# Moving the range check of 16 weight pieces from the last layer into attention

## The chip, the cores and the metric

The kernel runs on one core of a Trainium2 chip. The time is the device time of one execution in microseconds, as the median of several runs. TensorE does the matrix products, VectorE, ScalarE (ACT in the profile) and GpSimd (POOL) work on elements, and SyncE (SP) issues nearly all transfers between HBM and the chip's memory (SBUF).

## What is computed

Three layers, one behind the other, on 4 x 576 tokens of width 512. The weights w_in and w_out of the last one arrive as float64.

```
# 1. attention: 4 batches, 8 heads, head_dim 64; heads 0-3 see the last 32 keys,
#    heads 4-7 every fourth key of the last 128
scores = where(mask, q @ k.T / 8, -1e9);  x = softmax(scores) @ v
# 2. soft mixture of 8 experts, 4 slots each
logits = x @ phi
slots  = softmax(logits, over tokens).T @ x
out_e  = relu(slots_e @ w1[e]) @ w2[e]
x = softmax(logits, over slots) @ out
# 3. the layer the change is about: w_in 512 x 2048, w_out 2048 x 512
h = x @ w_in;  y = (h - tanh(h)) @ w_out
```

## The kernel before, in words

**Pieces.** w_in and w_out are cut into 16 pieces each, i0 to i15 and o0 to o15: 128 x 512 float64 words, 512 KB. A piece is loaded raw and turned into float32 by three steps on its raw bits: `top` (L276) and `low` (L273), on GpSimd or ScalarE, write the two halves of each word into the piece's place in SBUF; `merge` (L281, VectorE) joins them with bits of the raw word. Both `top` and `low` must be done before `merge`.

**Attention** (`attention`, to about 125 us) goes over 38 batches of four score blocks. Batch k runs `scores(k)`: sixteen matmuls (L466), then mask and row maximum (L470) and subtraction (L474, L477) on VectorE; one batch later `flip` transposes it on TensorE (L485) and ScalarE takes the exponential; another batch later come the product with v (L496) and, on VectorE, `norm` (L512 to L528). `turn` (TensorE, L382 and L394) and `regroup` (GpSimd, L331) prepare q and k of later heads, `shift_v` (GpSimd, L361) v; the logits of layer 2 are summed on VectorE (L430, L432). The order is written out by hand, and each engine takes its instructions in that order.

The first 16 pieces, PRE = i0, o0, i1, ... o7, are prepared in here, one per two batches: in batch 2n piece n is asked for, `top` and `low` follow in batch 2n + 4, and `merge` at the head of batch 2n + 6, ahead of that batch's mask. Their raw words lie in three buffers (`rawx`), so the load of piece n + 3 waits until piece n is merged. Their places are in `pre`. Two places in the loop close a pool and load weights w1, w2 into the room: the first one once all turns of q, k and e are done, the second in batch 36.

**Dispatch, experts and combine** (to about 200 us) stream 32 MB of w1 and w2.

**The last layer** (`second`) is ordered by a planner (`Plan`): every step has an engine, a guessed time and its predecessors, and the steps are written out in the order of the planned starts. It prepares the other 16 pieces and runs eight phases of products over 18 tiles of 128 tokens: h (L1109), its square (L1113, ScalarE), the product r (L1120 on VectorE, or L1124 and L1128 over ScalarE and GpSimd), and the accumulation into acc (L1082).

**The range check.** The fast way is right only for weights within a range. `check` (L890, L892) goes over the top 16 bits of each word of a raw piece and collects a mark: one 128 x 512 array `seen`. At the end `sift`, `marks` and `judge_o` turn it into part of a flag; if the flag is set, a general path (`any_size`) computes the last layer anew. Two pieces, i8 and i9, are checked behind their merge in the last layer. The raw words of the other 30 are gone by then, so the planner loads them a second time (into 12 buffers of the pool `raw`) and checks them one after another. Each check reads the `seen` that the one before wrote.

## Time and profile before

| | |
|---|---|
| median of three runs | 315.47 us (313.72 to 318.79) |
| the profiled execution, its own time | 317.44 us |
| its span, first to last instruction | 315.6 us |
| TensorE busy | 288.0 us, 91% |
| VectorE busy | 223.4 us, 71% |
| ScalarE busy | 157.6 us, 50% |
| GpSimd busy | 150.8 us, 48% |
| loads of raw pieces | 62, of 512 KB each |
| read from HBM | 80.64 MB |

One execution is profiled. PE is TensorE's matmul, PEld its weight load, DVE is VectorE. "a<-b x3" names what is written and read, and how often; "idle before" is the time an engine stood still ahead of the instruction, with what ended it. Matmuls overlap and their ends are modelled, so TensorE's busy time is not its work at full speed. Timeline rows are start us, us, engine, line, operation, [idle before]. Rows of windows give the stretch, its length, the busy us (instructions) of PE, PEld, DVE, ACT and POOL, then PEclk, the clock granted to TensorE as a share of full speed, the DMA engines' busy share and GB/s. Rows of groups end with "busy us, mean ns of one | idle before".

### The profile page before, as it was taken

Reading aid. Unit: us, or ns where it says so; the run is one execution under the profiler, and the core shown is the slowest. Engines: PE = TensorE matmul, PEld = TensorE weight load, DVE = VectorE, ACT = ScalarE, POOL = GpSimd, SP = SyncE. Lnnn points to the kernel's source line nnn. Section 1 sums busy time; section 2 is a strip of 40 time slices with the busy share of each in tenths; the row PEclk is TensorE's granted clock in tenths of the full one; section 3 lists DMA queues with packets and bytes.
Section 4 is the critical chain, followed back from the end, with each engine's and each line's share of the span. In section 5 each row is a group of like instructions: output and inputs, shape, how many; then the busy total and the mean of one; then the engine's idle time right before and its main releaser. Section 6 shows DMA issues by size and latency. Waiting matters only on the chain.

```text
span 315.6 us, 7494 instructions
## 1 busy us (share of the span) xinstructions
PE 288.0 (91%) x2674; PEld 200.0 (63%) x2674; DVE 223.4 (71%) x729; ACT 157.6 (50%) x298; POOL 150.8 (48%) x218
## 2 busy tenths in 40 slices
PE   5899998998899999889999697899999999999990
PEld 3688886786687866644432144556775788787860
DVE  4468896874879886608520026799889998999980
ACT  3366564544263356312310017689785735778630
POOL 8648757755678660010507006979534112433310
PEclk9999999999999999999999899699999999999997
DMA  7989899879797899978999999999445989613004
GB/s 194 257 222 348 227 326 344 267 224 310 235 330 243 287 339 412 384 262 321 374 334 410 409 379 367 387 380 353 158 135 194 312 273 346 207 61 104 31 1 143
DMA packets 61644, 85.93 MB, mean 272 GB/s; under 512 B 18976, under 2 KB 47008, under 8 KB 61600
## 3 DMA queue, kind: packets, MB, share of 16 engines
q1 hardware_dynamic: 60512, 85.12, 80.4%
q8 instruction: 23, 0.38, 0.5%
q10 hardware_dynamic: 1088, 0.26, 0.4%
q14 instruction: 21, 0.17, 0.2%
HBM read 80.64 MB, written 4.72 MB: 270 GB/s over the span
## 4 chain that ended last, share of the span: by engine, by line
PE 51%; DMA 25%; DVE 10%; POOL 5%; ACT 3%; issue 3%; SPq 1%; ACTq 0%; POOLq 0%
PE acc L1082 21%; DMA raw_i<-in_moe_w_in 10%; DMA raw_o<-in_moe_w_out 6%; DMA w<-in_moe_w 6%; PE h L1109 5%; PE sc L466 3%; PE hp L821 2%; PE pv L496 2%; PE pp L485 2%; DVE sm L470 2%; DVE pre L281 2%; POOL pre L273 2%; DMA q<-in_q 2%; POOL pre L276 1%; PE sp L743 1%
## 5 line engine op out<-in xcount | busy, mean ns | idle before, releaser
L1082 PE MATMUL acc<-wh,r 128*128 128x512 f32 x288 | 78.6, 398 | 0.7 <-DVE r L1120 0.7
L1113 ACT ACTIVATE u<-h,co 128x512 f32<-128x512 f32 (+1 forms) x80 | 49.2, 647 | 25.1 <-PE h L1109 20.0
L1082 PEld LDWEIGHTS acc<-wh,r 128*128 128x128 f32 x288 | 53.2, 189 | 13.3 <-issue 2.1
L1128 POOL TENSOR_TENSOR r<-d,u 128x512 fp32r<-128x512 f32 (+1 forms) x22 | 28.8, 1307 | 49.0 <-ACT d L1124 21.3
L1120 DVE SCALAR_TENSOR_TENSOR r<-h,co,u 128x512 fp32r<-128x512 f32 (+1 forms) x58 | 38.4, 691 | 2.6 <-PE acc L1082 1.5
L466 PE MATMUL sc<-kT,qT 64*64 64x96 f32 (+1 forms) x608 | 34.2, 252 | 0.7 <-DVE kT L403 0.4
L470 DVE CUSTOM_DVE_ANT_0 sm<-sc,m_sb 128x96 f32<-128x96 f32 x144 | 29.2, 257 | 7.7 <-PE sc L466 7.7
L486 ACT ACTIVATE pT<-pp 96x512 f32<-96x512 f32 x38 | 23.1, 609 | 21.4 <-PE pp L485 21.4
L466 PEld LDWEIGHTS sc<-kT,qT 64*64 64x64 f32 x608 | 26.9, 133 | 5.0 <-issue 1.8
L361 POOL TENSOR_SCALAR vw<-vw 32x256 f32<-32x256 f32 (+1 forms) x40 | 27.2, 680 | 4.8 <-DMA vw<-in_v 1.4
L1109 PE MATMUL h<-cT,Gs 128*128 128x512 f32 (+1 forms) x80 | 28.6, 394 | 0.5 <-DVE r L1120 0.4
L485 PE MATMUL pp<-c_sb,sm 128*96 128x128 f32 x152 | 23.7, 278 | 3.9 <-DVE sm L474 2.5
L496 PE MATMUL pv<-vw,pT 97*64 97x65 f32 x608 | 26.1, 227 | 0.1
L496 PEld LDWEIGHTS pv<-vw,pT 97*64 97x64 f32 x608 | 20.8, 137 | 7.8 <-issue 6.4
L821 PE MATMUL hp<-w,phi_sb 128*32 128x512 f32 x120 | 22.0, 614 | 3.7 <-DMA w<-in_moe_w 3.3
L404 ACT COPY qT<-tr_q 128x512 f32<-128x512 f32 x16 | 13.6, 853 | 23.5 <-PE tr_q L394 23.5
L474 DVE TENSOR_TENSOR sm<-sm,mx 128x384 f32<-128x384 f32 (+1 forms) x38 | 22.9, 602 | 1.2
L822 DVE COPY store<-hp 128x512 f32<-128x512 f32 x8 | 5.5, 690 | 23.9 <-PE hp L821 17.2
L485 PEld LDWEIGHTS pp<-c_sb,sm 128*96 128x96 f32 x152 | 15.9, 126 | 8.0 <-DVE sm L474 3.4
L420 ACT COPY xT<-xt 128x512 f32<-128x512 f32 (+1 forms) x19 | 14.5, 788 | 11.6 <-PE xt L411 11.0
L1109 PEld LDWEIGHTS h<-cT,Gs 128*128 128x128 f32 x80 | 15.1, 191 | 7.4 <-DVE r L1120 2.4
L822 ACT COPY store<-hp 128x512 f32<-128x512 f32 x8 | 4.7, 583 | 25.8 <-PE hp L821 25.8
(212 smaller groups left out, 513.7 us busy)
## 6 DMA issues: line engine op xcount, KB each, us to landing
w<-in_moe_w SPq DMA_DIRECT2D x58, 512.0 KB, 8.1
raw_o<-in_moe_w_out SPq DMA_DIRECT2D x32, 512.0 KB, 6.6
raw_i<-in_moe_w_in SPq DMA_DIRECT2D x30, 512.0 KB, 7.5
q<-in_q SPq DMA_DIRECT2D x16, 256.0 KB, 5.2
k<-in_k SPq DMA_DIRECT2D x16, 256.0 KB, 5.2
out<-X SPq DMA_DIRECT2D x14, 256.0 KB, 4.4
X<-in_moe_w SPq DMA_DIRECT2D x6, 512.0 KB, 7.1
vw<-in_v SPq DMA_DIRECT2D x16, 144.0 KB, 4.5
```

Of the source, the lines that this page charges most:

```text
L361: copy = lambda dst, src: nc.gpsimd.tensor_scalar(out=dst, in0=src, scalar1=1.0, scalar2=0.0, op0=ALU.mult, op1=ALU.add)
L466: nc.tensor.matmul(dst[half, lo:hi], lhsT=qT[u % NQ][half, i:i + QB], rhs=keys[half], start=True, stop=True)
L470: nc.vector.tensor_tensor_reduce(out=sm[:, o:o + n, :].rearrange("p g k -> p (g k)"), in0=sc[:, o:o + n, :].rearrange("p g k -> p (g k)"), ...
L485: nc.tensor.transpose(pp[:, i, :], sm[:, i, :], ident)
L486: nc.scalar.activation(out=pT[0:KB], in_=pp, func=AF.Exp, scale=0.125)
L496: nc.tensor.matmul(pv[64 * ab:64 * ab + 64, i, :], lhsT=pT[:, o + x, 64 * ab:64 * ab + 64], rhs=w[:, ab, u % 2, j + x, :], start=x == 0, s ...
L821: nc.tensor.matmul(hp[32 * dc:32 * dc + 32, :], lhsT=siT[:, dc, :], rhs=w_sb[8 * e + dc][:, 512 * hf:512 * (hf + 1)], start=True, stop=Tru ...
L1082: nc.tensor.matmul(live[key], lhsT=lhsT(), rhs=rhs(), start=new, stop=n == due)
L1109: nc.tensor.matmul(live["h", key], lhsT=Gs[:, 128 * f:128 * (f + 1)], rhs=cT[:, c0:c0 + w], start=True, stop=True)
L1113: nc.scalar.activation(out=live["u", key], in_=live["h", key], func=AF.Square, scale=co[:, SC, f:f + 1])
L1120: nc.vector.scalar_tensor_tensor(out=live["r", key], in0=live["h", key], scalar=co[:, BB, f:f + 1], in1=live["u", key], op0=ALU.add, op1=A ...
L1128: nc.gpsimd.tensor_tensor(out=live["r", key], in0=live["d", key], in1=live["u", key], op=ALU.mult)
```

## The change

The 16 pieces of PRE are checked in attention, each directly behind its merge and from the raw words that lie there. `check` moves out of `second` and is shared; the two places that call it in the last layer stay. The planner leaves out what was counted already: 16 of the 30 second loads and 16 of the 30 checks. The operation on a piece is the same, except that the first one of all is now i0 and no longer i8.

The mark needs a place before `chk` exists. `places` is a list of buffers; a check writes the newest and reads the one that the check before wrote. The first buffer is the place of the last piece, o7, which is filled only in batch 34. When the first pool is closed in the loop, a buffer of 1 KB per partition (`seen`, in a new pool between `wright` and the next weights) takes over, and in `second` the old one in `chk`.

```diff
@@ -280,6 +280,20 @@
         hi = raws[piece].bitcast(I32).rearrange("p (x two) -> p x two", two=2)[:, :, 1]
         nc.vector.scalar_tensor_tensor(out=w, in0=hi, scalar=3, in1=w, op0=ALU.logical_shift_left, op1=ALU.bitwise_xor)
 
+    places, counted = [], []
+
+    def marked(pool):
+        places.append(pool.tile([128, 512], U16, name=f"seen{len(places)}"))
+        return places[-1]
+
+    def check(piece):
+        x = quarter(piece, 3, U16)
+        if not counted:
+            nc.vector.tensor_scalar(out=places[-1], in0=x, scalar1=0x7800, scalar2=0x3800, op0=ALU.bitwise_and, op1=ALU.bitwise_xor)
+        else:
+            nc.vector.scalar_tensor_tensor(out=places[-1], in0=x, scalar=0x3800, in1=counted[-1][1], op0=ALU.bitwise_xor, op1=ALU.bitwise_or)
+        counted.append((piece, places[-1]))
+
     x0 = ctx.enter_context(tc.tile_pool(name="x0p", bufs=1)).tile([128, 2, NB, DM // 2], F32, name="X0")
     octx = ExitStack()
     xpool = octx.enter_context(tc.tile_pool(name="xpool", bufs=1))
@@ -566,6 +580,7 @@
                         later.append((u + 5, nm))
                 return done
 
+            places.append(place(PRE[-1]).bitcast(U16)[:, 0:512])
             load_qk(0, "e", nc.scalar)
             load_qk(0, "q")
             load_qk(0, "k")
@@ -615,11 +630,14 @@
                 n = k_ // 2
                 if k_ % 2 == 0 and 0 <= n - 3 < len(PRE):
                     merge(PRE[n - 3])
+                    check(PRE[n - 3])
                 if k_ % 2 == 0 and 0 <= n < len(PRE):
                     w_in_out(PRE[n], rawx.tile([128, 512], I64, tag="x", name=f"raw_{PRE[n][0]}{PRE[n][1]}"))
                 for at, cx, n in ((None, rctx, 4), (6 + 2 * (len(PRE) - 1), xctx, 3)):
                     if k_ > 0 and len(early0) == (at is not None) and (not ms and not qk and not later and not [e for e in extras if e[2] is turn] if at is None else k_ >= at):
                         cx.close()
+                        if at is None:
+                            marked(wctx.enter_context(tc.tile_pool(name="seen", bufs=1, side="right", reuse_waits="tile")))
                         early0.append(mctx.enter_context(tc.tile_pool(name=f"early{n}", bufs=n, side="right", reuse_waits="tile")))
                         for _ in range(n):
                             w_load(early0[-1])
@@ -879,18 +897,10 @@
         batches = [[0], [1], [2, 3, 4], [5, 6, 7], [8, 9, 10], [11, 12, 13], [14, 15]]
         joints = [[0], [1], [2, 3, 4], [5, 6, 7], [8, 9, 10], [11, 12, 13, 14, 15]]
         flat = x0.rearrange("p r j d -> p (r j d)")
-        seen = chk.tile([128, 512], U16, name="seen")
-        counted = []
+        seen = marked(chk)
 
         def load(piece):
             w_in_out(piece, raw.tile([128, 512], I64, tag="raw", name=f"raw_{piece[0]}{piece[1]}"))
-
-        def check(piece):
-            if not counted:
-                nc.vector.tensor_scalar(out=seen, in0=quarter(piece, 3, U16), scalar1=0x7800, scalar2=0x3800, op0=ALU.bitwise_and, op1=ALU.bitwise_xor)
-            else:
-                nc.vector.scalar_tensor_tensor(out=seen, in0=quarter(piece, 3, U16), scalar=0x3800, in1=seen, op0=ALU.bitwise_xor, op1=ALU.bitwise_or)
-            counted.append(piece)
 
         for piece in loads[:RAW]:
             load(piece)
@@ -1256,7 +1266,7 @@
 
         ck = None
         for piece in PRE + loads:
-            if piece in counted:
+            if piece in [x[0] for x in counted]:
                 continue
             key = ("raw", ("again", piece))
             ld = add(one("DMA", DMA, lambda piece=piece: load(piece)), deps=[P["mg", loads[-1]]], take=[key])
```

## Rows read from the trace of the kernel before

**Rows 1.** Windows by stretch, busy us (instructions), PEclk, DMA share, GB/s

```profile
26.00:118.00 92.00, 87.73 (x1326) 69.93 (x1320) 73.41 (x373) 46.32 (x94) 65.66 (x103) 1.00 0.92 288
...
140.00:150.00 10.00, 10.00 (x88) 3.95 (x86) 6.54 (x13) 2.38 (x4) 1.31 (x4) 1.00 0.75 271
...
160.00:180.00 20.00, 16.66 (x107) 5.22 (x104) 2.41 (x6) 1.55 (x3) 5.86 (x14) 0.97 1.00 383
...
200.00:210.00 10.00, 9.23 (x42) 6.47 (x43) 8.35 (x16) 7.45 (x15) 7.67 (x10) 0.86 1.04 391
210.00:220.00 10.00, 9.52 (x48) 6.63 (x47) 9.84 (x18) 8.00 (x14) 9.36 (x15) 1.00 1.05 364
...
250.00:260.00 10.00, 10.00 (x47) 8.16 (x46) 9.53 (x16) 4.50 (x8) 2.62 (x2) 1.00 0.93 293
```

**Rows 2.** Chain of waits in order of time: start, us, what

```profile
272.42 2.31 PE acc L1082 x10
```

**Rows 3.** Groups of TensorE's matmuls by line and shape, 248 to 307 us

```profile
L1082 PE MATMUL acc<-wh,r 128*128 128x512 f32 x190 | 50.9, 394 | 0.0
L1109 PE MATMUL h<-cT,Gs 128*128 128x512 f32 x37 | 14.0, 404 | 0.0
L1082 PE MATMUL acc<-Ms,cT 128*128 128x512 f32 x18 | 5.8, 401 | 0.0
```

**Rows 4.** The checks from 220 us on: two groups, then the first one

```profile
L892 DVE SCALAR_TENSOR_TENSOR seen<-raw_o,seen 128x512 uint16<-128x512 uint16 x16 | 16.2, 1015 | 0.3
...
L892 DVE SCALAR_TENSOR_TENSOR seen<-raw_i,seen 128x512 uint16<-128x512 uint16 x14 | 10.9, 778 | 0.2
...
226.47 0.68 DVE L892 SCALAR_TENSOR_TENSOR seen<-raw_i,seen 128x512 uint16<-128x512 uint16 x1
```

**Rows 5.** VectorE's waits, 26 to 118 us: total us, times, longest

```profile
DVE pre L281 <- POOL pre L273: 12.3, 9, 3.3
```

**Rows 6.** Timeline of all engines around one merge, 76 to 80 us

```profile
76.93 0.69 DVE L281 SCALAR_TENSOR_TENSOR pre<-raw_i,pre 128x512 int32<-128x512 int32 x1 [3.34 <-POOL pre L273]
76.97 1.13 POOL L331 TENSOR_SCALAR qm<-q 128x512 f32<-128x512 f32 x1
...
77.54 0.25 DVE L470 CUSTOM_DVE_ANT_0 sm<-sc,m_sb 128x96 f32<-128x96 f32 x1
...
78.07 0.62 POOL L331 TENSOR_SCALAR km<-k 128x512 f32<-128x512 f32 x1
...
78.81 0.47 DVE L477 TENSOR_SCALAR sm<-sm,mx 128x192 f32<-128x192 f32 x1
...
79.33 0.17 PEld L485 LDWEIGHTS pp<-c_sb,sm 128*96 128x96 f32 x2 [0.22 <-DVE sm L477]
```

**Rows 7.** Timelines of VectorE, then TensorE's weight loads, at three merges

```profile
28.67 0.72 DVE L474 TENSOR_TENSOR sm<-sm,mx 128x384 f32<-128x384 f32 x1
...
39.71 0.56 DVE L474 TENSOR_TENSOR sm<-sm,mx 128x384 f32<-128x384 f32 x1
...
117.74 0.42 DVE L432 TENSOR_TENSOR LT<-LT,lp 128x256 f32<-128x256 f32 x1
...
30.21 0.45 PEld L485 LDWEIGHTS pp<-c_sb,sm 128*96 128x96 f32 x4
...
40.38 0.39 PEld L485 LDWEIGHTS pp<-c_sb,sm 128*96 128x96 f32 x4
...
118.21 0.42 PEld L411 LDWEIGHTS xt<-c_sb,X 128*128 128x128 f32 x4 [0.65 <-DVE LT L432]
```

**Rows 8.** Timeline of VectorE, then of GpSimd, at 270 to 280 us

```profile
277.68 2.39 DVE L892 SCALAR_TENSOR_TENSOR seen<-raw_i,seen 128x512 uint16<-128x512 uint16 x2
...
273.87 1.30 POOL L1128 TENSOR_TENSOR r<-d,u 128x512 fp32r<-128x512 f32 x1 [1.54 <-ACT d L1124]
277.69 1.83 POOL L1128 TENSOR_TENSOR r<-d,u 128x512 fp32r<-128x512 f32 x1 [2.52 <-ACT d L1124]
```

**Rows 9.** Timeline of SP's queue, 80 to 90 us

```profile
84.56 0.38 SPq L251 DMA_DIRECT2D raw_o<-in_moe_w_out  x1
```

## The prediction

> **What bounds the kernel now.** I read the page's busy shares first, then the windows by stretch, then the chain of waits, and last the timeline around single merges.
>
> On the page TensorE is busy for 91% of the span and VectorE for 71% (the table above). The average hides three stages. In attention (26 to 118 us) TensorE is busy for 87.73 of 92 us and VectorE for 73.41, so VectorE has 18.6 us to spare; the DMA engines are at 0.92 [rows 1]. In the experts' stretch the transfers of weights set the pace: at 160 to 180 us the DMA engines are full and TensorE idles for 3.3 of 20 us [rows 1]. In the last layer (from 200 us) VectorE looks like the limit, with 9.84 of 10 us busy at 210 to 220 us and 9.53 at 250 to 260, but at 250 to 260 TensorE has no gap at all [rows 1].
>
> Whether TensorE is really full there, its busy time can't say, since the ends of matmuls are modelled. The chain of waits can: ten accumulating matmuls take 2.31 us, 0.231 each [rows 2]. Between 248 and 307 us there are 190 + 37 + 18 of that width [rows 3]; 245 x 0.231 is 56.6 us, and 8 half-wide ones and three small groups add about 1.5. That is 58.1 of 59 us. So the last layer is bound by TensorE's own work to within 1 us, and after the last matmul only copies and stores follow.
>
> In attention the order is another. A batch goes scores (TensorE), mask, maximum and subtraction (VectorE), transpose (TensorE), and TensorE has only about one batch of other work between. What VectorE puts ahead of a batch's mask is on TensorE's path as soon as the slack of that batch is used up. The merges sit exactly there.
>
> **The change, part by part.**
>
> *Removed from the last layer: 16 checks.* The 30 checks there take 16.2 + 10.9 us [rows 4], 0.90 each, so 16 are 14.5 us of VectorE. The first of them runs at 226.5 us [rows 4]. By then TensorE is full, and the most that shorter waits can give back is the 1.0 us of bubbles found above. I take 0.5, the middle of 0 and 1.0.
>
> *Removed: 16 loads of 512 KB*, 8.4 MB on SP's queue. They are issued behind all first-time loads and share the queue with the stores of the outputs; 14 loads of the same kind remain and fill the same buffers first. No TensorE work waits for them. Cost nothing, gain nothing; it would be a gain only if a first-time load or one of the last stores stood behind them.
>
> *Moved: the mark.* Three buffers and no copy: each check writes the newest buffer and reads the one before. No instruction is added. The new 1 KB buffer lies between two pools of weights and shifts the later ones by 1 KB, so that a weight load may wait for another old tile; all those tiles come free in the same two batches. Nothing.
>
> *Added to attention: 16 checks*, each right behind a merge. No row of attention has a check. The nearest row is the merge itself, which has the same form (scalar_tensor_tensor, two inputs in SBUF, 128x512): it starts at 76.93, and the next VectorE instruction at 77.54 [rows 6], so 0.61 us is the low price. The high price comes from GpSimd. Its qm copy, started in the middle of that merge, takes 1.13 us, where the same copy of km behind it takes 0.62 [rows 6]. In the last layer two checks run back to back from 277.68 and take 2.39 us, with a GpSimd multiply beside them that takes 1.83, against 1.30 for one without [rows 8]. So the first check holds the multiply up for 0.5 us, and then the multiply holds the second check for about 1.1 us. A check behind a merge is this second one whenever GpSimd has work waiting, and it mostly has: the helper's next copy starts within 0.1 us of the merge in ten cases. The copy ends at 78.10, 0.56 after the merge, so the high price is 0.61 + 0.54 = 1.15 us. I take 0.88, midway, since GpSimd is busy for 65.66 of 92 us [rows 1] and not every check finds it pending.
>
> The Trainium skill says this as a rule (SBUF — State Buffer, "Who interferes with whom"): a VectorE instruction with two SBUF inputs and a GpSimd instruction that reads SBUF exclude each other, and the later one waits for the whole of the earlier one. The two checks at 277.68 agree. By the rule alone every check would have the high price, the third rival below.
>
> *What of it reaches TensorE.* For each of the 16 merges I compared the end of the batch's last VectorE step with the start of the TensorE step that reads it. At 39.71 + 0.56 = 40.27 the subtraction ends and its transpose loads at 40.38: 0.11 us of slack [rows 7]. At 78.81 + 0.47 = 79.28 the transpose follows at 79.33 [rows 6]. At the last merge it is the logits' sum, 117.74 + 0.42 = 118.16, against 118.21 [rows 7]. Eleven merges are tight like this (at 37.8, 43.2, 50.0, 61.3, 76.9, 83.3, 89.9, 95.0, 105.6, 110.3 and 115.8 us), with 1.18 us of slack in all. The other five have 0.7 to 1.0; the first is 28.67 + 0.72 = 29.39 against 30.21, 0.82 [rows 7].
>
> At 0.61 the tight ones cost 11 x 0.61 - 1.18 = 5.5 us and the others nothing. At 1.15 they cost 11.5, and the others 1.4 beyond their slack: 12.9. At 0.88 it is 8.5 + 0.3 = 8.8 us.
>
> Against that stands what can absorb it. VectorE waits 12.3 us in front of nine merges for GpSimd's two steps of the same piece [rows 5], which wait for the piece's transfer. If that chain (SP's queue, the transfers, GpSimd) keeps its own pace, a batch that is late simply waits less at the next such merge. In the limit only the last merge's cost is left, 0.6 us. But the chain doesn't run free: SP also waits for buffers that TensorE and GpSimd release, and GpSimd loses 0.5 us to each check. I take half of 8.8 us, 4.4, and keep 0.6 to 12.9 for the range.
>
> *Who waits for the waiting instruction.* Behind the check on VectorE stand the masks, the normalization and the copies of logits. SP waits for the check where it waited for the merge, since the raw buffer comes free 0.6 us later; the next load into it is issued 7 to 14 us after the merge in all thirteen cases (the merge at 76.93 ends at 77.62 [rows 6], the load at 84.56 [rows 9]), so that costs nothing. If SP ran closer, each load would go 0.6 us later.
>
> *What follows attention.* The weights of the experts are loaded into places that dispatch and the experts release, and the DMA engines are at 0.75 at 140 to 150 us [rows 1], so they can't run ahead: I pass the delay on in full.
>
> *Sum.* The profiled execution took 317.44 us, 1.84 more than its span. 317.44 + 4.4 - 0.5 = 321.3. It lies 1.97 above the median of the three runs, so on the median's scale the forecast is 319.4 us, 1.2% above 315.47. Two per cent, about what a measurement of this kernel can tell from no change, is 6.3 us.
>
> **The rivals.**
>
> *The waits absorb it.* The transfers keep their own pace, and every late batch is caught at the next merge that waits for GpSimd. For it: nine such waits, the longest 3.34 us [rows 6], and DMA engines at 0.92. Against it: three of the last eight merges have no such wait, and GpSimd is itself pushed. It gives a slip of 0.6 to 2.7 us; with 1.5 and 0.5 back, 316.5.
>
> *Nothing absorbs it.* The copies behind a late GpSimd hold up SP's loads of q and k, these the next raw piece, and the whole chain moves with VectorE, at the high price: 12.9 - 0.5, 327.9 us. For it: the checks at 277.68 and GpSimd at 71% busy. Against it: VectorE's 18.6 us to spare.
>
> *Faster: the last layer gives back more than attention pays.* The place is 200 to 220 us, where TensorE is short of 0.77 and 0.48 us [rows 1] with VectorE at 9.84 of 10. If the planner, freed of 16 checks, puts the products r earlier there, those 1.25 us and the 1.0 us of bubbles come back; with a slip of 0.6 us that is -1.7, 313.8 us. It decides from the point at which the slip is under 2.3 us. Against it: no removed check runs before 226.5 us [rows 4].
>
> *The change doesn't do what it says.* The first mark lies in the place of piece o7, which GpSimd fills in batch 34. The move depends on the last turn of q, k and e, which the code's order puts into batch 32, so batch 33 switches and batch 34's check already writes the second buffer. Were the move a batch later, the mark would hold foreign words, the flag would be set, and the general path would run: its 864 products alone are 864 x 0.231 = 200 us more, over 510 us.
>
> **How the numbers follow.** Forecast (net +2 to +8 us) 0.50; absorbed (-0.5 to +2) 0.22; nothing absorbs (+8 to +13) 0.15; faster 0.11; mark lost 0.02. The range 313.0 to 325.0 takes in the forecast, the absorbed case, most of the faster one and the lower end of the unabsorbed. Slower by over 2% (over 321.8 us, net over 6.3): a fifth of the forecast, 0.10, and 0.15 and 0.02: 0.27. Faster by over 2% would need 6.3 us, which no case but a rest of the third reaches: 0.04. Within: 0.69.
>
> **What would show it.** In the profile after: 16 checks on VectorE between 26 and 120 us, those behind a merge with GpSimd pending at 1.1 us or more, the others at 0.7; longer GpSimd copies; longer waits of transposes for VectorE; the last scores some 4 us later; 46 instead of 62 loads of pieces; VectorE below 9 of 10 from 230 us while the matmuls there keep their 0.231 us. I am wrong if the last scores come at the old time, if the stretch from 220 us to the last matmul shortens by more than 1.4 us, or if the experts' stretch swallows the delay.

## The result and the profile after

The changed kernel takes 319.31 us, the median of five runs (318.67 to 322.37); the kernel before takes 315.47 us in five runs timed beside it (313.72 to 318.79). The ratio is 1.0147 with a 95% interval of 1.0108 to 1.0186: 3.4 to 5.9 us slower, clear of the scatter and inside the two per cent. The profiled execution of the changed kernel is its slowest run, 322.37 us with a span of 320.6.

The windows by stretch of the changed kernel, with the columns of [rows 1]:

```profile
26.00:118.00 92.00, 83.51 (x1267) 67.24 (x1265) 87.21 (x371) 43.61 (x90) 66.13 (x102) 1.00 0.91 279
...
210.00:220.00 10.00, 9.15 (x50) 5.70 (x48) 9.63 (x21) 8.87 (x16) 7.63 (x14) 1.00 1.06 378
250.00:260.00 10.00, 10.00 (x44) 7.74 (x43) 9.90 (x15) 6.16 (x11) 1.50 (x1) 1.00 0.12 46
...
280.00:290.00 10.00, 10.00 (x43) 7.70 (x42) 7.70 (x17) 6.58 (x11) 2.73 (x3) 1.00 0.00 0
290.00:300.00 10.00, 10.00 (x45) 7.86 (x44) 6.72 (x19) 7.77 (x14) 3.90 (x3) 1.00 0.33 107
```

In attention VectorE's busy time rises from 73.41 to 87.21 us of 92, and TensorE's falls from 87.73 to 83.51: TensorE now waits where VectorE waited. At 250 to 260 us nothing has changed: TensorE has no gap, and VectorE is at 9.90 with the checks that are left. Only from 280 us is VectorE below 8 of 10, and TensorE has no gap there either.

The groups of VectorE's instructions in attention, 20 to 124 us, that belong to a merge (L281) or to a check:

```profile
L294 DVE SCALAR_TENSOR_TENSOR pre<-raw_o,pre 128x512 uint16<-128x512 uint16 x7 | 7.9, 1126 | 0.0
L281 DVE SCALAR_TENSOR_TENSOR pre<-raw_i,pre 128x512 int32<-128x512 int32 x8 | 6.8, 854 | 0.0
L294 DVE SCALAR_TENSOR_TENSOR pre<-raw_i,pre 128x512 uint16<-128x512 uint16 x6 | 6.7, 1110 | 0.0
L281 DVE SCALAR_TENSOR_TENSOR pre<-raw_o,pre 128x512 int32<-128x512 int32 x8 | 6.3, 783 | 0.0
...
L292 DVE TENSOR_SCALAR pre<-raw_i 128x512 uint16<-128x512 uint16 x1 | 1.0, 1000 | 0.0
...
L294 DVE SCALAR_TENSOR_TENSOR seen<-raw_i,pre 128x512 uint16<-128x512 uint16 x1 | 0.7, 684 | 0.0
L294 DVE SCALAR_TENSOR_TENSOR seen<-raw_o,seen 128x512 uint16<-128x512 uint16 x1 | 0.7, 683 | 0.0
```

Sixteen checks take 16.9 us, 1.06 each, against the 0.88 that the forecast took. Four of them (74.02, 80.17, 116.47 and 121.47 us) take 0.68 or 0.69, the low price; one takes 0.88, and eleven take 1.00 to 1.53. The four are just those at whose start no GpSimd instruction was running; at the other twelve one was. The timeline of all engines at one merge shows why:

```profile
59.70 0.68 DVE L281 SCALAR_TENSOR_TENSOR pre<-raw_o,pre 128x512 int32<-128x512 int32 x1
59.86 1.16 POOL L273 TENSOR_SCALAR pre<-raw_i 128x512 int16<-128x512 uint16 x1
...
60.30 1.20 DVE L294 SCALAR_TENSOR_TENSOR pre<-raw_o,pre 128x512 uint16<-128x512 uint16 x1
...
61.11 1.13 POOL L375 TENSOR_SCALAR vw<-vw 32x256 f32<-32x256 f32 x2
...
61.43 0.24 DVE L484 CUSTOM_DVE_ANT_0 sm<-sc,m_sb 128x96 f32<-128x96 f32 x1
```

GpSimd's `low` step starts during the merge and runs to 61.02. The check, which has the form of the merge and could run in 0.68 us, ends only at 61.50, half a microsecond behind GpSimd, and the mask (L484) that TensorE needs starts only at 61.43, 1.73 us after the merge began. In [rows 6] it started 0.61 us after.

Who waits for that? TensorE's weight loads, 20 to 124 us of the changed kernel (total us, times, longest):

```profile
PEld pp L499 <- issue: 4.3, 5, 1.6
PEld pp L499 <- DVE sm L488: 3.9, 4, 1.6
PEld xt L425 <- DVE LT L444: 1.3, 1, 1.3
PEld pp L499 <- PE sc L480: 1.1, 1, 1.1
PEld pp L499 <- DVE sm L491: 0.9, 1, 0.9
...
PEld pp L499 <- PE xt L425: 0.5, 1, 0.5
```

and 20 to 120 us of the kernel before:

```profile
PEld pp L485 <- DVE sm L474: 3.4, 3, 1.6
PEld pp L485 <- PE tr_q L394: 1.2, 1, 1.2
...
PEld pp L485 <- issue: 0.8, 2, 0.4
PEld pp L485 <- PE sc L466: 0.7, 2, 0.4
PEld xt L411 <- DVE LT L432: 0.7, 1, 0.7
```

With the rows below 0.5 us the transposes (pp and xt) wait 12.2 us in all against 7.7, and the 4.5 us between them are as much as the slip of this pair of profiles. In the second pair it is 9.3 against 6.3, 3.0 us of a slip of 5.9; TensorE's busy time in attention is 3.1 us longer there, at a lower granted clock (last section). VectorE's waits for GpSimd ahead of the merges, 12.3 us in [rows 5], are gone altogether: the changed kernel has not one.

In the last layer, the groups of matmuls of the changed kernel from 253 to 312 us are those of [rows 3]:

```profile
L1092 PE MATMUL acc<-wh,r 128*128 128x512 f32 x190 | 50.9, 393 | 0.0
L1119 PE MATMUL h<-cT,Gs 128*128 128x512 f32 (+1 forms) x45 | 16.5, 385 | 0.0
L1092 PE MATMUL acc<-Ms,cT 128*128 128x512 f32 x18 | 5.7, 396 | 0.0
```

The second group holds eight half-wide products too ("+1 forms"), so that it is 37 wide ones as in [rows 3]. The checks that are left there:

```profile
L294 DVE SCALAR_TENSOR_TENSOR seen<-raw_o,seen 128x512 uint16<-128x512 uint16 x8 | 8.0, 1001 | 0.1
L294 DVE SCALAR_TENSOR_TENSOR seen<-raw_i,seen 128x512 uint16<-128x512 uint16 x6 | 5.2, 868 | 0.1
```

They are 14. Their means, 1.00 and 0.87 us, are about those of [rows 4], 1.015 and 0.778, so a check there has not become cheaper: 13.2 us remain of 27.1, and some 14 us are gone. The last one starts at 279.2 us instead of 299.7. The loads of pieces fall from 62 to 46, and the data read from HBM from 80.64 to 72.25 MB.

The parts of each profiled execution, in us. *Attention* runs from batch 4's first scores to the start of the last sum of logits, *experts* from there to the copy of the experts' last product (191 us in the profile of before), *middle* to the first product of `msum`, *last* from there to the end of the last product into `acc`. *Waits* are VectorE's for GpSimd ahead of merges between 26 and 118 us, *VectorE* its busy time in those 92 us.

| kernel | its time | attention | experts | middle | last | waits | VectorE | checks in the last layer |
|---|---|---|---|---|---|---|---|---|
| before | 317.44 | 106.3 | 64.2 | 48.6 | 67.60 | 12.3 | 73.41 | 30 |
| before, again | 316.21 | 105.0 | 63.4 | 48.7 | 67.61 | 12.3 | 74.21 | 30 |
| after | 322.37 | 110.8 | 62.7 | 49.4 | 67.28 | 0 | 87.21 | 14 |
| after, again | 322.65 | 110.9 | 64.4 | 48.9 | 67.31 | 0 | 85.83 | 14 |
| no_checks | 314.87 | 102.0 | 64.3 | 49.6 | 67.30 | 4.3 | 78.28 | 14 |
| no_checks, again | 316.34 | 104.7 | 64.0 | 49.7 | 67.31 | 4.5 | 78.11 | 14 |
| both | 321.75 | 109.9 | 64.0 | 48.2 | 67.63 | 0 | 87.46 | 30 |
| twice | 334.58 | 122.7 | 63.4 | 49.6 | 67.26 | 0 | 87.21 | 14 |
| check_first | 318.07 | 107.8 | 63.0 | 48.2 | 67.26 | 1.3 | 86.23 | 14 |
| tail | 319.22 | 105.9 | 64.2 | 49.4 | 67.26 | 2.7 | 86.52 | 14 |
| one_input | 314.51 | 104.0 | 63.4 | 49.2 | 67.27 | 2.5 | 84.43 | 14 |
| tight11 | 316.20 | 106.9 | 63.1 | 48.6 | 67.30 | 1.6 | 83.09 | 19 |
| loose5 | 315.57 | 104.1 | 62.7 | 49.4 | 67.65 | 4.2 | 82.52 | 25 |

Two columns move with the change: attention by +4.5 us in the first pair of profiles and +5.9 in the second, and *last* by -0.32 and -0.30. The other two scatter by 1 to 2 us without order.

How the slip grows can be followed at the merges. This is how far each merge of the changed kernel is behind that of the kernel before, both counted from their first merge, in us, for the first pair of profiles and for the second:

| merge | 1 | 2 | 4 | 6 | 8 | 9 | 10 | 12 | 14 | 16 |
|---|---|---|---|---|---|---|---|---|---|---|
| first pair | 0 | 0.97 | 2.72 | 3.17 | 4.10 | 1.44 | 2.32 | 2.78 | 4.00 | 3.83 |
| second pair | 0 | 0.11 | 2.98 | 4.65 | 5.49 | 3.33 | 4.86 | 4.72 | 6.00 | 5.29 |

The slip is made in steps, and at the ninth merge 2.7 and 2.2 us of it vanish. That merge is the one at 76.93 us in [rows 6], where VectorE of the kernel before waits 3.34 us for GpSimd: the late kernel simply doesn't wait there.

### The profile page after: what moved, and what is told of

Read it like the earlier page. It is cut to its first block, busy times and chain, and to the rows that moved or that the text cites. A ratio compares the mean times of both kernels' runs of the same rounds, so it can differ in the third digit from the quotient of the medians.

```text
span 320.6 us, 7445 instructions
## 1 busy us (share of the span) xinstructions
PE 289.1 (90%) x2674; PEld 202.1 (63%) x2674; DVE 230.2 (72%) x729; ACT 157.7 (49%) x298; POOL 151.0 (47%) x218
## 3 DMA queue, kind: packets, MB, share of 16 engines
HBM read 72.25 MB, written 4.72 MB: 240 GB/s over the span
## 4 chain that ended last, share of the span: by engine, by line
PE 59%; DVE 16%; DMA 14%; ACT 3%; issue 2%; POOL 1%; SPq 1%; ACTq 0%; DVEq 0%
PE acc L1092 21%; DMA w<-in_moe_w 6%; PE h L1119 5%; PE sc L480 5%; DMA vw<-in_v 4%; PE pv L510 4%; DMA raw_i<-in_moe_w_in 3%; PE pp L499 3%; DVE pre L294 3%; DVE sm L484 3%; DVE pre L281 3%; DVE sm L488 2%; PE xt L425 2%; PE hp L839 2%; PE tr_k L408 2%
## 5 line engine op out<-in xcount | busy, mean ns | idle before, releaser
L1138 POOL TENSOR_TENSOR r<-d,u 128x512 fp32r<-128x512 f32 (+1 forms) x22 | 27.4, 1245 | 51.5 <-ACT d L1134 21.8
L484 DVE CUSTOM_DVE_ANT_0 sm<-sc,m_sb 128x96 f32<-128x96 f32 x144 | 29.1, 256 | 7.9 <-PE sc L480 7.8
L375 POOL TENSOR_SCALAR vw<-vw 32x256 f32<-32x256 f32 (+1 forms) x40 | 24.9, 623 | 4.7 <-DMA vw<-in_v 2.0
L488 DVE TENSOR_TENSOR sm<-sm,mx 128x384 f32<-128x384 f32 (+1 forms) x38 | 25.0, 657 | 1.2
L839 PE MATMUL hp<-w,phi_sb 128*32 128x512 f32 x120 | 20.1, 597 | 4.1 <-DMA w<-in_moe_w 3.7
L840 DVE COPY store<-hp 128x512 f32<-128x512 f32 x8 | 5.5, 690 | 22.4 <-PE hp L839 17.2
L276 POOL TENSOR_SCALAR pre<-raw_o 128x512 bf16<-128x512 int16 x16 | 13.9, 880 | 8.9 <-issue 4.6
```

The lines of the kernel that those rows point to most:

```text
L375: copy = lambda dst, src: nc.gpsimd.tensor_scalar(out=dst, in0=src, scalar1=1.0, scalar2=0.0, op0=ALU.mult, op1=ALU.add)
L484: nc.vector.tensor_tensor_reduce(out=sm[:, o:o + n, :].rearrange("p g k -> p (g k)"), in0=sc[:, o:o + n, :].rearrange("p g k -> p (g k)"), ...
L488: nc.vector.tensor_tensor(out=sm[:, o:o + n], in0=sm[:, o:o + n], in1=mx[:, o:o + n].unsqueeze(2).to_broadcast([128, n, KB]), op=ALU.subtract)
L839: nc.tensor.matmul(hp[32 * dc:32 * dc + 32, :], lhsT=siT[:, dc, :], rhs=w_sb[8 * e + dc][:, 512 * hf:512 * (hf + 1)], start=True, stop=Tru ...
L1138: nc.gpsimd.tensor_tensor(out=live["r", key], in0=live["d", key], in1=live["u", key], op=ALU.mult)
```

## The experiments

Each edit is made to the changed kernel. A ratio is to the kernel before, timed beside it on the same chip; 0.001 is 0.315 us.

**no_checks: the 16 checks left out, all else as changed.** The 16 pieces of PRE are neither checked nor loaded again.

```diff
-    places, counted = [], []
+    places, counted, skipped = [], [], []
...
-                    check(PRE[n - 3])
+                    skipped.append(PRE[n - 3])
...
-            if piece in [x[0] for x in counted]:
+            if piece in [x[0] for x in counted] + skipped:
```

> The kernel after, with the 16 checks in attention left out (so these 16 pieces are not range-checked at all); buffers of the mark, shifted pools, the 14 remaining second loads and checks all as after. Theory (the checks in attention are the whole cost, the last layer gives nothing back since TensorE is full there): attention as before, last scores near 119 us, VectorE again waiting some 12 us for GpSimd in front of the merges, msum to last accumulation 67.2 +- 0.5 us, and 315.5 us in all, ratio 0.997 to 1.003. Rival 1 (the 1 KB shift of the pools or the buffers cost the time): stays at 318 to 319 us. Rival 2 (the last layer does give back the 14.5 us of VectorE in part, hidden behind a dearer attention): 311 to 314 us.

Measured: 314.19 us (12 runs), ratio 0.9962 (0.9925 to 1.0). Without its checks the changed kernel is no slower than the kernel before. So the mark's new places, the 1 KB shift of the pools and the missing loads cost nothing that shows, and by the ratios the checks in attention cost 1.0147 - 0.9962, 5.8 us (4.1 to 7.5). Two things that were expected didn't come: VectorE waits 4.3 us for GpSimd, not 12, and attention takes 102.0 us, not 106 (see no_checks_again). The result is also the upper bound of what any place for these checks could gain: 1.2 us, with an interval from 0 to 2.4.

**both: checks in attention, and the old ones of the last layer kept.** All 30 loads and checks of the last layer stand again.

```diff
-            if piece in [x[0] for x in counted]:
+            if piece in [x[0] for x in counted if x[0] not in PRE]:
```

> The kernel after, with the 16 second loads and 16 checks of the last layer put back, so those pieces are checked twice. Theory: the last layer is full of TensorE's own work with or without them, so the time stays that of after, 319 to 320 us (ratio 1.012 to 1.018), and msum to last accumulation stays 67.2 +- 0.5 us. Rival 2 (the last layer gave back some of attention's cost): 2 to 4 us slower than after, 321 to 323 us.

Measured: 320.28 us (6 runs), ratio 1.0143 (1.0083 to 1.0204). The cost in attention is there in full, and the time can't be told from the changed kernel's. The finer number is in the profiles: *last* is 67.63 us here, 67.60 and 67.61 before, and 67.26 to 67.31 in the eight profiles with 14 checks; the means are 67.61 and 67.28. Sixteen loads of 512 KB and some 14 us of VectorE are worth 0.33 us at the end.

**twice: the check run two times behind each merge.** The second one repeats the first.

```diff
+                    check(PRE[n - 3])
                     check(PRE[n - 3])
```

> The kernel after, with each of the 16 checks in attention made twice in a row. Theory: in the kernel after, VectorE is busy for 87.2 of 92 us between 26 and 118 us and no longer waits for GpSimd, so the absorbing waits are used up and nearly every further check lengthens attention by its own 0.6 to 0.7 us (the second one less often meets a waiting GpSimd copy): 16 x 0.6 = 10 us more, 327 to 331 us, ratio 1.035 to 1.05. Rival (half of it is absorbed as before): another 4 to 5 us, 323 to 325 us.

Measured: 334.62 us (6 runs), ratio 1.061 (1.0552 to 1.0668). That is more than the theory gave: 14.3 us over "both" on the same chip, 0.9 for each of the second sixteen checks, where the first sixteen cost 5.8 us, 0.36 each. The groups of checks in its attention, 20 to 140 us:

```profile
L294 DVE SCALAR_TENSOR_TENSOR pre<-raw_i,pre 128x512 uint16<-128x512 uint16 x13 | 13.6, 1042 | 0.2
L294 DVE SCALAR_TENSOR_TENSOR pre<-raw_o,pre 128x512 uint16<-128x512 uint16 x14 | 13.0, 928 | 0.2
```

The price of a check has not risen (1.04 and 0.93). What has changed is that nothing absorbs it: VectorE is busy for 87.21 of 92 us with or without the second sixteen. The waits for GpSimd were used up by the first. The profiles say the same: all checks in attention take 30.3 us here and 17.5 in "both", and the 12.8 us between them are just what attention grows by, from 109.9 to 122.7. TensorE's granted clock is 0.94 in those 92 us of twice (last section), so a part of the 14.3 us can be the clock's.

**before_again and after_again: a second profile of each kernel.** No edit, on one chip.

> The kernel before, unchanged, profiled once more. Without the checks attention took 102.0 us from batch 4's scores to the last logits sum, against 106.3 in the first profile of before, with 4.3 us instead of 12.3 of waits for GpSimd ahead of the merges, although its instructions are the same up to batch 33. Theory (these waits differ from execution to execution with the transfers): somewhere between 102 and 107 us, the waits between 4 and 13 us, and the last layer 67.2 to 67.7 us from msum to the last accumulation. Rival (the change made attention itself shorter in some other way): 106 us again, 12 us of waits.

> The kernel after, unchanged, profiled once more, since its first profile was its slowest run. Theory: attention 108 to 111 us, no wait for GpSimd ahead of a merge or under 1 us, checks of 1.0 to 1.1 us mean, last layer 67.2 to 67.7 us. Rival (the first profile was an outlier of the mechanism too): waits for GpSimd again, attention below 107 us.

Measured: 316.21 and 322.65 us, the parts in the table. The kernel before lies within its theory's wide ranges, but at the rival's end: 105.0 us of attention with 12.3 us of waits in ten merges. The changed kernel has its theory's case, no waits and 110.9 us. Attention is 5.9 us longer, *last* 0.30 us shorter. The checks cost about the same (7.9 us for seven and 7.2 for six).

**check_first: the check ahead of the merge.**

```diff
-                    merge(PRE[n - 3])
                     check(PRE[n - 3])
+                    merge(PRE[n - 3])
```

> The kernel after, with each check directly ahead of its merge instead of behind it. The check needs only the raw words, so it can run while the merge would still wait for GpSimd's second step. Theory (the price is what VectorE adds behind GpSimd's step): part of it falls into time in which VectorE would wait, the merge is then the second instruction that meets GpSimd's next copy, and the slip is 1 to 3 us smaller than after: 316.5 to 318.5 us. Rival (VectorE is simply full, and the order of two neighbours changes nothing): 319 to 320 us.

Measured: 319.89 us, ratio 1.0111 (1.0044 to 1.0178). The interval, 1.4 to 5.6 us, is too wide to tell the theories apart. What the order does is plain in the groups, 20 to 140 us:

```profile
L281 DVE SCALAR_TENSOR_TENSOR pre<-raw_o,pre 128x512 int32<-128x512 int32 x8 | 8.0, 996 | 0.0
L281 DVE SCALAR_TENSOR_TENSOR pre<-raw_i,pre 128x512 int32<-128x512 int32 x8 | 7.0, 880 | 1.3 <-POOL pre L273 1.3
L294 DVE SCALAR_TENSOR_TENSOR pre<-raw_o,pre 128x512 uint16<-128x512 uint16 x7 | 5.7, 821 | 0.0
L294 DVE SCALAR_TENSOR_TENSOR pre<-raw_i,pre 128x512 uint16<-128x512 uint16 x6 | 4.4, 731 | 0.0
```

The checks fall to 0.82 and 0.73, and the merges rise from 0.78 and 0.85 to 1.00 and 0.88: so the later of the two mostly pays, whichever it is. Whether the order is worth something is not settled.

**one_input: an instruction with one input in the place of the check.** A maximum over the high words of the raw piece, 512 per partition as in the check, into a column of its own. The range of 16 pieces is not checked.

```diff
+    tops = const.tile([128, 16], F32, name="tops")
...
-                    check(PRE[n - 3])
+                    skipped.append(PRE[n - 3])
+                    nc.vector.tensor_reduce(out=tops[:, n - 3:n - 2],
+                        in_=raws[PRE[n - 3]].bitcast(F32).rearrange("p (x two) -> p x two", two=2)[:, :, 1],
+                        axis=AX.X, op=ALU.max)
```

> The kernel after, with each check in attention replaced by a maximum over the 512 high words of the piece, an instruction of the same length with one input in SBUF instead of two (so these 16 pieces are not range-checked). Theory (more than a third of the price is waiting for GpSimd's copy, because both inputs lie in SBUF): each takes 0.6 to 0.7 us even where a GpSimd copy is pending, 10 to 11 us in all instead of 17.0, GpSimd's copies behind it are no longer stretched, and the time falls to 315.5 to 317.5 us. Rival (the two engines don't exclude each other, the check is just slower in attention): about 1.06 us each and 318.5 to 320 us.

Measured: 315.82 us (12 runs), ratio 1.0032 (1.0 to 1.0064). Its groups in attention, then one of them in the timeline:

```profile
L635 DVE TENSOR_REDUCE tops<-raw_o 128x1 f32<-128x512 f32 x8 | 5.4, 677 | 0.0
L635 DVE TENSOR_REDUCE tops<-raw_i 128x1 f32<-128x512 f32 x8 | 5.4, 676 | 0.0
```

```profile
60.84 0.68 DVE L281 SCALAR_TENSOR_TENSOR pre<-raw_i,pre 128x512 int32<-128x512 int32 x1
60.99 1.00 POOL L346 TENSOR_SCALAR qm<-q 128x512 f32<-128x512 f32 x1
...
61.44 0.68 DVE L635 TENSOR_REDUCE tops<-raw_i 128x1 f32<-128x512 f32 x1
...
61.96 0.62 POOL L346 TENSOR_SCALAR km<-k 128x512 f32<-128x512 f32 x1
```

GpSimd's `qm` copy starts in the middle of the merge, as in [rows 6], and is stretched to 1.00 us. But the instruction behind the merge starts at 61.44 all the same and takes 0.68 us beside it. All sixteen take 0.67 to 0.68 us, thirteen of them with a GpSimd instruction beside them, 10.8 us in all against 16.9, and GpSimd's `low` steps keep 0.80 and 0.82 us where the changed kernel has 0.97 and 1.01. Over no_checks it costs 0.0070, 2.2 us (about 0.7 to 3.7), so some 3.6 of the checks' 5.8 us go with the check and GpSimd holding each other up, and 2.2 remain without it. The maximum differs from the check in more than its one input (it is a reduction, on float32), so the run shows that the form of the instruction decides; it doesn't show that the number of inputs does (last section).

**tail: the check at the end of its batch's work.** Behind the normalization of the batch instead of ahead of its masks. The load into the raw buffer is asked for there too.

```diff
-                    check(PRE[n - 3])
-                if k_ % 2 == 0 and 0 <= n < len(PRE):
+                    if n - 3 == 15:
+                        check(PRE[n - 3])
+                if k_ % 2 == 0 and 0 <= n < 3:
...
+                n = k_ // 2
+                if k_ % 2 == 0 and 0 <= n - 3 < 15:
+                    check(PRE[n - 3])
+                if k_ % 2 == 0 and 3 <= n < len(PRE):
+                    w_in_out(PRE[n], rawx.tile([128, 512], I64, tag="x", name=f"raw_{PRE[n][0]}{PRE[n][1]}"))
```

> The kernel after, with each check behind the normalization of its batch instead of behind the merge (the last piece's stays), and the raw buffer's next load asked for there. Theory (the price is what VectorE puts ahead of a tight batch's mask): the batch's transposes no longer wait for the check, only the next batch's mask does, which has no merge in front; 315.5 to 317.5 us. Rival (VectorE is full, 87 of 92 us, so the place within two batches doesn't matter): 318.5 to 320 us.

Measured: 317.29 us (12 runs), ratio 1.0054 (1.0022 to 1.0085). The checks there, 20 to 140 us:

```profile
L294 DVE SCALAR_TENSOR_TENSOR pre<-raw_o,pre 128x512 uint16<-128x512 uint16 x7 | 5.7, 819 | 0.0
...
L294 DVE SCALAR_TENSOR_TENSOR pre<-raw_i,pre 128x512 uint16<-128x512 uint16 x6 | 4.1, 681 | 0.0
```

A check away from the merge is mostly not stretched (0.68 for the pieces i; all sixteen take 12.0 us against 16.9), and it no longer stands ahead of its own batch's masks. Which of the two helps more, the run doesn't separate. The checks cost 2.9 us over no_checks, half as much, and the kernel is still 1.7 us slower than the kernel before.

**tight11 and loose5: the forecast's list of merges put to the test.** In tight11 only the eleven merges that the forecast called tight have a check; the other five pieces are checked in the last layer as before. In loose5 it is the other way round, and the mark of those five is dropped when the buffer changes.

```diff
-                    check(PRE[n - 3])
+                    if n - 3 in (2, 3, 4, 6, 8, 9, 10, 11, 13, 14, 15):
+                        check(PRE[n - 3])
```

```diff
-        if not counted:
+        if not counted or (len(places) > 1 and counted[-1][1] is places[0]):
...
-                    check(PRE[n - 3])
+                    if n - 3 in (0, 1, 5, 7, 12):
+                        check(PRE[n - 3])
```

> The kernel after, with only eleven of the 16 checks in attention: those of the merges that the prediction called tight (0.05 to 0.3 us of slack before TensorE's next step). The other five pieces are loaded again and checked in the last layer, as before. Theory of the prediction (the tight ones carry nearly all of the cost): 318.5 to 319.5 us, as after. Rival (the five loose ones cost as much each, since VectorE as a whole is full and the slack read from the trace before is gone as soon as the first checks shift it): 11 of 16 of the 5 us, 317 to 318 us.

> The kernel after, with only the five checks of the merges that the prediction called loose (0.7 to 1.0 us of slack); the other eleven pieces are loaded again and checked in the last layer. The mark of these five is dropped when the mark changes buffers, so that they don't count in the flag. Theory of the prediction: nothing, 314 to 315 us, as without checks. Rival (each check costs the same): 5 of 16 of the 5 us, 315.5 to 316 us.

Measured: tight11 317.15 us (12 runs), ratio 1.0063 (1.0031 to 1.0094); loose5 315.81 us (12 runs), ratio 1.0047 (1.0016 to 1.0077). Over no_checks the eleven cost 3.2 us, 0.29 each, and the five 2.7 us, 0.54 each, both with some 1.5 us of uncertainty. Against the kernel before, on the same chip, they are 2.0 us (1.0 to 3.0) and 1.5 us (0.5 to 2.4). The five were to cost next to nothing, and the eleven as much as all sixteen. The theory of the list falls: the loose ones are not free. How much dearer or cheaper than a tight one they are is not settled: 0.4 us of the five's 2.7 are the last layer's with its 25 checks (67.65 us against 67.28), no_checks was timed on another chip, and its one execution on this chip (below) took 316.34 us, longer than loose5's median.

**no_checks_again: a second profile of no_checks**, because the first had only 4.3 us of waits where the kernel before has 12.3.

> The kernel without the checks in attention (so 16 pieces are not range-checked), profiled once more. Its attention took 102.0 us with 4.3 us of waits for GpSimd, against 105.0 and 106.3 with 12.3 in two profiles of before, with the same instructions up to batch 33. Theory (scatter between executions): 102 to 106 us. Rival (something in the changed program makes attention 3 to 4 us shorter each time): 102 again, with 4 us of waits.

Measured: 316.34 us. VectorE's waits for GpSimd ahead of merges, 26 to 118 us, in the first profile of no_checks:

```profile
DVE pre L281 <- POOL pre L273: 4.3, 4, 2.0
```

The second has 4.5 us, which is the rival's case, so the shorter waits are not the scatter of one execution. But its attention takes 104.7 us, which is the theory's. The chain of waits by line, 26 to 118 us, for the kernel before, for no_checks and for the changed kernel, in this order:

```profile
by line: DMA raw_i<-in_moe_w_in 24.0%; DMA raw_o<-in_moe_w_out 16.4%; DVE sm L470 6.5%; DVE pre L281 5.7%; POOL pre L273 5.7%; DMA q<-in_q 5.7%; PE sc L466 5.4%; POOL pre L276 5.1%; PE pp L485 4.0%; DVE sm L474 4.0%; PE pv L496 3.3%; issue 
```

```profile
by line: PE sc L480 22.7%; PE pv L510 17.0%; PE pp L499 14.5%; PE xt L425 7.1%; PE tr_q L408 6.4%; PE tr_k L408 4.8%; POOL vw L375 3.0%; DMA vw<-in_v 2.7%; PE lp L441 2.7%; PE tr_e L396 2.5%; DVE sm L488 2.4%; DVE sm L484 2.1%; issue 1.8%; 
```

```profile
by line: DMA vw<-in_v 14.8%; DVE pre L294 9.7%; PE sc L480 9.6%; DVE sm L484 9.4%; PE pv L510 8.8%; DVE pre L281 8.1%; DVE sm L488 8.1%; PE pp L499 7.1%; PE xt L425 4.7%; DVE X L542 3.4%; PE tr_k L408 3.3%; PE tr_q L408 2.6%; issue 2.5%; PE
```

Before, 40% of the chain are transfers of raw pieces (also in the second profile, 29.6% and 10.4%). In no_checks it is TensorE's own work, scores, products with v and transposes (54.2% in the first three entries, 61.8% in the second profile). In the changed kernel the pieces' transfers are not among the entries, VectorE's merges, checks, masks and normalization have 38.7% (44.9% in the second profile), and TensorE's entries that are shown 36.1%. Releasers are inferred, so the shares are rough, but what stands in front differs in the three: transfers of pieces, TensorE's own work, and VectorE and TensorE in turn.

## Why the forecast came out as it did

**The last layer is full with TensorE's own work: right.** The argument from 0.231 us per product and the count of products gave at most 1.0 us back, 0.5 taken. "both" and the table show 0.33. The rival that saw 200 to 220 us as the place of a gain falls with it: *middle* is 49.4 and 48.9 us after against 48.6 and 48.7 before.

**The price of a check: the mechanism right, the size too low.** 0.88 was taken between 0.61 and 1.15, because not every check would find GpSimd pending. Measured are 1.06 on average, 0.68 without and mostly 1.20 with GpSimd pending, and twelve of sixteen are nearer the high price. That GpSimd is the cause is shown twice: the four cheap checks are the four that found no GpSimd instruction running, and in one_input an instruction of another form takes 0.677 in the same places. The rule of the Trainium skill (SBUF — State Buffer, "Who interferes with whom") that the forecast quotes, a two-input VectorE instruction and a GpSimd instruction that reads SBUF excluding each other, agrees with this trace: 1.20 us against 0.68. The case with the high price, which the forecast once calls the third rival, is the second in its list. Two of its readings are slightly off and change nothing: GpSimd's next copy starts within 0.1 us of the merge in twelve cases, not ten, and the sum 0.61 + 0.54 should have the 0.56 us that were read.

**What reaches TensorE: the list of tight and loose merges fell.** This is the step of the forecast that failed. It compared, merge by merge, the end of VectorE's last step with TensorE's use of it in the trace of before, and took the eleven tight ones with 1.18 us of slack to carry 8.5 of the 8.8 us. tight11 and loose5 don't bear that out: the tight ones alone cost 3.2 us and not the whole 5.8, and the loose ones are not free. In the changed kernel the transposes of three loose merges wait for VectorE too (by 0.58 to 0.96 us), and some tight ones don't. The likely reason, which no run isolates, is that the checks ahead of a merge have already altered its slack; each row was right for its batch alone, with all others unchanged.

**Half of it absorbed: right in its sum, and by the mechanism named.** The forecast put the absorbing into VectorE's 12.3 us of waits for GpSimd and, for want of a reason for more, took half of 8.8 us. Measured: attention 4.5 us longer in the first profiles and 5.9 in the second, 4.4 forecast. Over the whole of attention (the column's stretch) VectorE's busy time grows by 18.8 us in the first pair, from 82.8 to 101.6, most of it the checks (16.9) and longer merges (1.3). Its idle time falls by 14.3 us, from 23.5 to 9.2, and 18.8 - 14.3 is 4.5; in the second pair it is 17.2 - 11.3. Most of the 14.3 are the 12.3 us of waits. The ninth merge shows the catching up itself, and twice shows what the next sixteen cost when nothing is left: VectorE stays at 87.21 of 92 us. The forecast's gross 8.8 us was too small, since it counted no cost at all for most of the loose merges and 0.88 for a check, and its half was too small a share to be absorbed; the two errors go against each other, and the 4.4 was in that measure lucky.

**"The waits absorb it", 316.5 us, and "nothing absorbs it", 327.9 us:** the first is right up to where the 12.3 us are spent; there are more checks than that. The second is what twice does.

**What costs nothing: right for the mark, the 1 KB and the loads; too sure of the raw buffers.** no_checks holds the mark's move, the 1 KB and the fewer loads together at -1.2 us (interval -2.4 to 0). Its raw buffers come free at the merge, so it says nothing of their later release. Before the change SP asked for each 7 to 14 us after the merge. In the changed kernel that distance is gone: the loads are issued 0.06 to 7.3 us behind the end of the check, and at 100.97 us SP stands waiting for one that ends at 100.91. Its queue, 26 to 125 us:

```profile
SPq L253 <- DVE pre L294: 0.7, 1, 0.7
```

No merge waits for GpSimd in the changed kernel, so none was held up by a late piece. What the 0.7 us cost the transfers behind it in the queue, no run separates.

**The experts' stretch passes the delay on: as far as can be told.** It takes 62.7 and 64.4 us after against 64.2 and 63.4 before; a delay that it swallowed would show as some 5 us.

**Of the signs to look for**, the last scores come 5.6 and 5.8 us later in the two pairs of profiles (4 forecast), and one sign was wrong: VectorE was to be below 9 of 10 from 230 us. It is at 9.90 at 250 to 260 us and stays below 9 only from 280. The planner brings the 14 checks that are left forward, as their last at 279.2 shows. It cost the forecast nothing, since TensorE is the limit there.

**What stays open.** Up to the change of buffers at batch 33, no_checks and the kernel before issue the same instructions on every engine in attention. Yet VectorE waits 12.3 us ahead of merges in both profiles of before and 4.3 and 4.5 in both of no_checks, its load of i4 is issued at 67.6 and 68.8 us against 69.7 and 70.0, and attention is 0.3 to 4.3 us shorter. The two profiles of no_checks are of two chips, so one chip isn't the cause; what it is these runs don't tell. Some of the 2.7 us between these two profiles can be the clock: in the second one 80 to 90 us are granted 0.83, worth at most 1.7 us. The 5.8 us of the checks are therefore counted against no_checks and the 4.6 against the kernel before, and a part of the 1.2 us between them can be this. 0.33 us of it are the last layer's.

No version tried that checks all the pieces beats the kernel before. The last layer has 0.33 us to give for some 14 us of VectorE, and the cheapest place tried for the sixteen checks in attention costs 2.9.

## What to carry to other kernels

Before work is moved off a busy engine, count what the engine behind it must do: products x 0.231 us filled the last layer to 1 us, so an engine at 9.8 of 10 was not its limit, and taking some 14 us off it gave 0.33. Slack read batch by batch from one trace doesn't add up, since each insertion uses slack that the next one counted on; compare the added time with the engine's idle time over the whole stretch, and expect the price of the next instruction to be full once that is spent (0.36 us each for the first sixteen, 0.9 for the next). Two VectorE instructions with two inputs back to back, with GpSimd at work, cost about half a microsecond more than their own time here (1.20 us for the second against 0.68); put other work between them, as tail does, or look for a form that isn't held up, as the maximum of one_input.

## What the runs showed of the hardware that was not expected

The granted clock of TensorE falls in attention in three of the thirteen profiles. In the kernel before it is 1.00 there [rows 1]. In the second profile of the changed kernel (first two rows), in twice (next two) and in the second profile of no_checks it has stretches below (columns as in [rows 1]):

```profile
40.00:50.00 10.00, 8.22 (x99) 6.46 (x97) 9.16 (x35) 4.17 (x7) 8.15 (x8) 0.74 1.04 321
50.00:60.00 10.00, 9.78 (x142) 8.03 (x140) 8.36 (x38) 5.20 (x11) 6.79 (x14) 0.92 1.06 326
40.00:50.00 10.00, 7.49 (x101) 6.05 (x100) 9.76 (x32) 3.68 (x7) 6.84 (x8) 0.86 1.03 320
60.00:70.00 10.00, 9.52 (x116) 7.97 (x116) 8.44 (x38) 4.83 (x11) 3.70 (x8) 0.83 0.78 233
80.00:90.00 10.00, 8.02 (x94) 6.62 (x93) 5.92 (x29) 3.15 (x7) 8.44 (x13) 0.83 0.85 266
```

A mean of 0.74 is about half of the ten microseconds at 1.2 GHz instead of 2.4. Each fall comes behind a standstill of TensorE that waits for VectorE, 1.73 to 2.51 us long. In the timeline, one in the second profile of the changed kernel, one in the second of no_checks, and one in twice:

```profile
43.98 0.61 PE L499 MATMUL pp<-c_sb,sm 128*96 128x128 f32 x4 [1.78 <-DVE rd L526]
84.72 1.06 PE L499 MATMUL pp<-c_sb,sm 128*96 128x128 f32 x4 [1.98 <-DVE rd L532]
75.82 0.66 PE L425 MATMUL xt<-c_sb,X 128*128 128x128 f32 x4 [2.25 <-DVE LT L444]
```

Behind the third one, of 2.25 us, the clock stays at 1.00 in twice, so a standstill alone doesn't decide. In the changed kernel the fall had no cost that shows: TensorE's busy time in attention is 104.6 us with it and 102.0 in the first profile, where the clock was 1.00 from 26 to 118 us, but attention took 110.9 us and 110.8. TensorE has so much less to wait there.

A check with one input, the first one (L292, a tensor_scalar), took 1.00 us beside a GpSimd copy and 0.42 in tight11, where no GpSimd instruction ran beside it (38.74 us); the maximum over as many words took 0.68 beside one. So one input alone doesn't decide; the runs don't show what in the form does.
